# Tiles of 32 queries for the second pair of heads in block 1's attention, and w_a and w_b packed in place

## The chip, the cores and the metric
One core of a Trainium2 chip runs the kernel. Its engines take their instructions each from a list of its own: PE (TensorE: matrix products and transposes), DVE (VectorE), ACT (ScalarE) and POOL (GpSimd); SP and POOL also issue transfers. The lists are fixed when the program is built, and an instruction waits until what it needs is done, and with it all that stand behind it in its list. The metric is the time of one execution on the device, in microseconds. The granted clock of PE was 0.999 of full speed in the profiled execution, which is the level of 2.4 GHz.

## The reference
```python
def _attn_ref(q, k, v):                      # (4, 8, 576, 64) each
    scores = scale * np.matmul(q, k.transpose(0, 1, 3, 2))
    mask_local = (rel >= 0) & (rel < stride)               # stride = 32, heads 0 to 3
    mask_strided = (rel >= 0) & (pos[None, :] % stride == pos[:, None] % stride)   # heads 4 to 7
    ...                                      # softmax over the masked scores, sum + 1e-9
    return np.matmul(attn, v)
def _moe_ref(x, w_in, w_out, s, b):          # x (2304, 512), w_in (512, 2048), w_out (2048, 512)
    r = np.maximum(x @ w_in, 0.0)
    return (s * (r * r) + b) @ w_out
def _moe2_ref(x, w_a, w_b, w_out):           # w_a, w_b (512, 1536), w_out (1536, 512)
    return ((x @ w_a) * (x @ w_b)) @ w_out
```
The three run one after the other. The weights come as doubles (64 bits); the kernel converts them to 32-bit floats.

## The kernel before
Tokens are cut into blocks; the first network runs block by block over 16 steps f of its hidden units. One step ("call") of block n issues on PE twelve matmuls for h of step f (`h_mm`, into one PSUM bank of the pool ps_h), twelve matmuls acc of an earlier step (`o_mm`), and then `attend`, which runs what is due of the attention of block n+1. Each product is made of three passes: both operands are split into a high half `[:, 0]` (written by ACT) and a low half `[:, 1]` (DVE's subtraction), both by `split`, L121 to L124. So after h of a step ACT does relu (L802), the square (L806) and the high half "hi" of gt (L122), DVE then the low half "lo" (L124), and acc of that step stands two calls later.

In block 0 the weights w_in and w_out are converted in the same calls: `to_float32` (L140) takes two 32-bit words for each number, in a tile `raw`: ACT scales the high words (L142), DVE shifts the low ones (L145), joins them (L148) and packs the result (L158); `split` makes the halves w.

The attention of a block has four parts: two pairs of local heads (a band of 32 keys) and two pairs of strided heads. Each is a generator of six or seven steps: loads, transposes of queries and keys, scores, softmax, transposes of the probabilities (ppt), products with v (po). `plan` (L1059) gives each step its call by a table; the call's number in block 0 is first + t. `attend` puts a step's PE work behind that call's acc; DVE's and ACT's parts are put in place by the scheduler. There are two forms of each kind. `local` (L289) and `strided` (L371) work in tiles of 64 queries and transpose queries and keys on PE (pst); a `local` call covers four or three tiles, so each pair needs two. `local_pairs` (L453) and `strided_pairs` (L513) work in tiles of 32 queries over the whole block, transpose on DVE, and have half as many columns in the strided softmax (288 against 576). Before, block 1's attention, which runs beside block 0 of the network (44 to 137 us), is all in the first form; the blocks behind it use the second.

The softmax of `local` in block 1 puts the mask in by a PE matmul (mask times ident_b) and takes the sum with the exponential on ACT (accum_out); the other forms add the mask on DVE and sum on DVE.

In blocks 1 to 3 `convert_w2` (L851) converts the 36 words of the second network's w_a, w_b and w_out, i = 0 to 35, kind i % 3: `to_float32` packs word i into a tile w2s (one buffer), POOL stores it to w2d[i] (L865) and then loads word i+2 (L130 for w_a and w_b, L135 for w_out) into the pool raw, which has two buffers.

Of the kernel before, what the change touches and what calls it, by code (L numbers as in the profile page):

```python
# [10 lines left out]
F32 = mybir.dt.float32  # L11
F32R = mybir.dt.float32r
U32 = mybir.dt.uint32
BF16 = mybir.dt.bfloat16
AF = mybir.ActivationFunctionType
ALU = mybir.AluOpType
AX = mybir.AxisListType
# [3 lines left out]
P = 128  # L21
# [6 lines left out]
def sparse_attention_two_mlps(  # L28
# [14 lines left out]
    nc = tc.nc  # L43
    B, H, S, D = q.shape
    NT, DM = out.shape
# [7 lines left out]
    TF = P  # L53
# [9 lines left out]
    scale = 1.0 / float(D) ** 0.5  # L63
# [5 lines left out]
    hp = ctx.enter_context(tc.tile_pool(name="hp", bufs=1))  # L69
# [11 lines left out]
    lp = att.enter_context(tc.tile_pool(name="lp", bufs=1, side="right"))  # L81
# [11 lines left out]
    w2s = [dram.tile([P, 2, 2, DM], F32, name=f"w2s{i}") for i in range(NF2)]  # L93
# [4 lines left out]
    def mm(*args, **kwargs):  # L98
        last_pe[:] = [nc.tensor.matmul(*args, **kwargs).ins]  # L99
# [40 lines left out]
    def to_float32(r, out=None, quarters=False):  # L140
        low, high = r[:, :, 0], r[:, :, 1]
        nc.scalar.activation(  # L142
            out=high.bitcast(F32), in_=high.bitcast(F32), func=AF.Copy, scale=HIGH_SCALE
        )
        nc.vector.tensor_scalar(  # L145
            out=low, in0=low, scalar1=29, scalar2=None, op0=ALU.logical_shift_right
        )
        nc.vector.scalar_tensor_tensor(  # L148
            out=low, in0=high, scalar=3, in1=low, op0=ALU.logical_shift_left, op1=ALU.bitwise_or
        )  # L150
        out = high if out is None else out
        pieces_ = [(out, high, low)]
        if quarters:
            to = out.rearrange("p (r a i c) -> p a r i c", r=2, a=2, c=STR)
            low, high = (t.rearrange("p (r i a c) -> p a r i c", r=2, a=2, c=STR) for t in (low, high))
            pieces_ = [(to[:, a], high[:, a], low[:, a]) for a in range(2)]
        for to, high, low in pieces_:
            nc.vector.scalar_tensor_tensor(  # L158
                out=to, in0=high, scalar=0x80000000, in1=low, op0=ALU.bitwise_and, op1=ALU.bitwise_or
            )  # L160
        return out.bitcast(F32)
# [24 lines left out]
    QT = 64  # L186
# [246 lines left out]
    def softmax_pairs(pt, pss, msk, cols):  # L433
        na = pt.shape[1]
        wide = msk[:, None, None, :].to_broadcast([P, na, 2, cols])
        for h, of in enumerate((pt[:, :, 0:4:3, 0:cols], pt[:, :, 1:3, 0:cols])):
            nc.vector.tensor_tensor(
                out=of, in0=pss[h].rearrange("p (a b) c -> p a b c", b=2), in1=wide, op=ALU.add
            )
        pt = pt.rearrange("p a x c -> p (a x) c")[:, :, 0:cols]  # L440
        mx = lp.tile([P, 4 * na], F32, tag="mx", name="mx", bufs=2)
        sm = lp.tile([P, 4 * na], F32, tag="sm", name="sm", bufs=2)
        wide = lambda t: t[:, :, None].to_broadcast(list(pt.shape))
        nc.vector.tensor_reduce(out=mx, in_=pt, op=ALU.max, axis=AX.X)
        nc.vector.tensor_tensor(out=pt, in0=pt, in1=wide(mx), op=ALU.subtract)
        nc.scalar.activation(out=pt, in_=pt, func=AF.Exp, scale=scale)
        yield
        nc.vector.tensor_reduce(out=sm, in_=pt, op=ALU.add, axis=AX.X)
        nc.vector.tensor_scalar_add(out=sm, in0=sm, scalar1=1e-9)
        nc.vector.reciprocal(out=sm, in_=sm)  # L450
        nc.vector.tensor_tensor(out=pt, in0=pt, in1=wide(sm), op=ALU.mult)

    def local_pairs(bb, n, pair):  # L453

        nt = TR // QS
        nu = -(-nt // 4)
        nq, nk = TR, TR + STR
        room = lp.tile([P, nq + nk], F32, tag="qk", name="qk")
        qk = room.rearrange("p (j c) -> p j c", c=STR)
        pt = room[:, 0:nu * 2 * PITCH].rearrange("p (a x c) -> p a x c", x=4, c=PITCH)  # L460
        blocks_load(qk, 0, q, bb, 2 * pair, TF, S)
        blocks_load(qk, nt, k, bb, 2 * pair, TF - STR, S)
        yield
        qkT = lp.tile([P, nq + nk], F32, tag="lT", name="qkT")
        qT, kT = qkT[:, 0:nq], qkT[:, nq:]
        with after(list(behind)):
            nc.vector.transpose(out=qkT.rearrange("p (j c) -> p j c", c=STR), in_=qk)
        yield
        vn = [lp.tile([P, m, D], F32, tag=tag, name="vn") for m, tag in ((8, "vn"), (nt - 8, "lpt"))]
        for h in range(2):  # L470
            at = v[bb, 2 * pair + h, TF - STR:S, :]
            for u in range(nu):
                m = min(4, nt - 4 * u)
                p0 = (h ^ u % 2) * WS
                src = bass.AP(at.tensor, at.offset + 4 * u * QS * D, [[D, WS], [QS * D, m], [1, D]])
                nc.sync.dma_start(out=vn[u // 2][p0:p0 + WS, u % 2 * 4:u % 2 * 4 + m], in_=src)
        pss = [ps_a.tile([P, nu, WS], F32, tag="a", name="pss") for _ in range(2)]
        for j in range(4 * nu):
            i = min(j, nt - 1) * QS
            for h in range(2):  # L480
                hr = slice(h * D, (h + 1) * D)
                mm(
                    pss[h][j % 4 * QS:(j % 4 + 1) * QS, j // 4],
                    lhsT=qT[hr, i:i + QS], rhs=kT[hr, i:i + WS], start=True, stop=True,
                )
        yield from softmax_pairs(pt, pss, masks[QS][0], WS)
        yield
        ppt = ps_a.tile([P, nu, P], F32, tag="a", name="ppt")
        for u in range(nu):
            mm_t(ppt[:, u], pt[:, u // 2, u % 2 * 2:u % 2 * 2 + 2].rearrange("p x c -> p (x c)"), ident)  # L490
        pT = lp.tile([P, nu, P], F32, tag="lT", name="pT")
        nc.scalar.activation(out=pT, in_=ppt, func=AF.Copy)
        yield
        po = [ps_a.tile([P, nu // 2, P], F32, tag="a", name="po") for _ in range(2)]
        for a in range(nu // 2):
            for jj in range(4):
                for b in range(2):
                    u, c = 2 * a + b, slice(jj * QS, (jj + 1) * QS)
                    j = 4 * u + jj
                    for h in range(2 * (j < nt)):  # L500
                        rows = slice((h ^ b) * WS, (h ^ b) * WS + WS)
                        mm(
                            po[b][h * D:(h + 1) * D, a, c], lhsT=vn[a][rows, j - 8 * a], rhs=pT[rows, u, c],
                            start=True, stop=True,
                        )
        xt, c0 = x_tile(n), first_column(n)
        for u in range(nu):
            c1 = c0 + u * P
            m = min(P, c0 + nq - c1)
            split(xt[:, 0, pair, c1:c1 + m], xt[:, 1, pair, c1:c1 + m], po[u % 2][:, u // 2, 0:m])  # L510
        yield
# [339 lines left out]
    def convert_w2():  # L851
        words = {}

        def load(i):
            if i < 3 * NF2:
                f, kind = divmod(i, 3)
                words[i] = stage((w_a, w_b, w_o2)[kind], f, kind < 2, raw, nc.gpsimd)[0]

        load(0)
        load(1)  # L860
        yield
        for i in range(3 * NF2):
            with after(list(behind)):
                w = to_float32(words.pop(i), hp.tile([P, DM], U32, tag="w", name="w2s"), i % 3 == 2)
            nc.gpsimd.dma_start(out=w2d[i], in_=w)  # L865
            load(i + 2)
            yield
# [189 lines left out]
    steps = {}  # L1057

    def plan(n):  # L1059
        at_f = (-3, 0, 1, 2, 4, 5) if n == 1 else (-3, 0, 1, 2, 3, 5)  # L1060
        if n == 1:
            near = [
                (4 * i - 1, local(0, n, i % 2, TF + i // 2 * 4 * QT, 4 - i // 2), (-2, 0, 1, 1, 2, 3, 4))
                for i in range(4)
            ]
        else:
            near = [(8 * i, local_pairs(n - 1, n, i), (-5, -1, 0, 1, 2, 4)) for i in range(2)]
        far = [(8 * i + 1, (strided if n == 1 else strided_pairs)(n - 1, n, i), at_f) for i in range(2)]
        if n == 1:
            near[0] = (0, near[0][1], (-5, -3, 0, 1, 1, 2, 3))  # L1070
            far[0] = (1, far[0][1], (-5, 1, 2, 3, 5, 7))
        if n == 2:
            near[0] = (0, near[0][1], (-4, -1, 0, 1, 2, 4))
        for first_, gen, at in near + far:
            for t in at:
                steps.setdefault((n - 1) * NF1 + first_ + t, []).append(gen)
# [510 lines left out]
```

## Time and profile before
| | |
|---|---|
| median of 3 runs | 881.11 us (880.87 to 881.37) |
| the profiled execution | 882.01 us, span 880.2 us |
| PE busy | 870.9 us, 99% |
| DVE, ACT, POOL busy | 679.1, 406.4, 158.1 us |
| mean DMA rate over the span | 213 GB/s |
| chain that ended last | PE 96%, ACT 2%, DVE 1% |

The profiled execution is one of its own, 0.90 us above the median of the timed ones. Busy PE time is modelled at the ends of matmuls, so starts are the better mark. Engines other than PE are busy for part of the span, and their idle time costs nothing as long as PE doesn't wait for them.

### The profile page before, as it was taken

How to read it: one execution, taken by the hardware profiler on the slowest of the kernel's cores; microseconds unless marked ns; L12 is line 12 of the kernel's file. 1: busy time of each engine (PE TensorE's matmuls, PEld its weight loads, DVE VectorE, ACT ScalarE, POOL GpSimd, SP SyncE). 2: the span in 40 equal slices, each digit the busy share in tenths (PEclk: the TensorE clock that was granted, in tenths of full speed). 3: DMA queues.
4: the chain of work that ended last, by engine and by line, in shares of the span. 5: the costliest groups of instructions: out<-in, count | busy, mean ns of one | idle time of the engine just before them, and what ended most of it. 6: DMA issues, size and time to landing. Idle time of an engine off the chain costs nothing.

```text
span 880.2 us, 17207 instructions
## 1 busy us (share of the span) xinstructions
PE 870.9 (99%) x6296; PEld 805.4 (92%) x6296; DVE 679.1 (77%) x1363; ACT 406.4 (46%) x872; POOL 158.1 (18%) x308
## 2 busy tenths in 40 slices
PE   8999999999999999999999999999999999999998
PEld 6778888999888899998888999999999999999998
DVE  6898996686767676847876798798877797887794
ACT  6777774443433343337665333463223463222261
POOL 6000001111112211114544000005400005200020
PEclk9999999999999999999999999999999999999999
DMA  9975543866685758458999668688668788766487
GB/s 213 289 236 151 173 85 105 186 163 165 170 201 151 178 173 188 140 169 281 351 317 338 197 207 261 216 256 263 203 198 278 251 252 260 211 200 206 150 259 217
DMA packets 173156, 187.21 MB, mean 213 GB/s; under 512 B 108880, under 2 KB 125648, under 8 KB 173072
## 3 DMA queue, kind: packets, MB, share of 16 engines
q1 hardware_dynamic: 147776, 119.90, 47.7%
q0 software_dynamic: 20096, 64.90, 22.4%
q10 hardware_dynamic: 5200, 1.31, 0.8%
q8 instruction: 50, 0.82, 0.4%
q14 instruction: 34, 0.28, 0.1%
HBM read 143.59 MB, written 42.47 MB: 211 GB/s over the span
## 4 chain that ended last, share of the span: by engine, by line
PE 96%; ACT 2%; DVE 1%; issue 0%; POOL 0%; ACTq 0%; POOLq 0%
PE pp L99 30%; PE h L99 23%; PE acc L99 22%; PE o L99 15%; PE po L99 2%; PE pss L99 1%; PE ppt L102 1%; PE fpo L99 1%; ACT fpt L620 1%; PE lull L99 0%; ACT raw L142 0%; PE fps L102 0%; PE pst L102 0%; ACT fqkT L620 0%; PE fpp L102 0%; PE fss L99 0%
## 5 line engine op out<-in xcount | busy, mean ns | idle before, releaser
L99 PE MATMUL pp<-x2w,wf 128*128 128x384 f32 x1296 | 230.9, 334 | 0.0
L99 PEld LDWEIGHTS pp<-x2w,wf 128*128 128x128 f32 x1296 | 225.2, 188 | 0.1
L99 PE MATMUL h<-x,w 128*128 128x512 f32 (+1 forms) x960 | 215.8, 373 | 0.0
L99 PE MATMUL acc<-gt,w 128*128 128x512 f32 (+2 forms) x960 | 210.7, 368 | 1.0 <-ACT w L122 1.0
L99 PEld LDWEIGHTS acc<-gt,w 128*128 128x128 f32 x960 | 175.5, 188 | 24.0 <-ACT w L122 1.4
L99 PEld LDWEIGHTS h<-x,w 128*128 128x128 f32 x960 | 172.5, 188 | 24.5 <-DVE w L124 0.5
L99 PE MATMUL o<-gf,o2w 128*128 128x384 f32 (+1 forms) x756 | 130.3, 333 | 0.7 <-issue 0.7
L99 PEld LDWEIGHTS o<-gf,o2w 128*128 128x128 f32 x756 | 129.6, 188 | 1.1 <-ACT gf L620 1.0
L802 ACT ACTIVATE r<-h 128x512 f32<-128x512 f32 (+1 forms) x80 | 44.3, 554 | 134.3 <-PE h L99 121.3
L620 ACT ACTIVATE gf<-quad 128x384 fp32r<-128x384 f32 x126 | 63.6, 522 | 84.4 <-DVE quad L625 61.6
L1343 POOL DMA_DIRECT2D out_dram<-ot x80 | 44.7, 567 | 249.4 <-DVE ot L1329 242.0
L625 DVE TENSOR_TENSOR gf<-quad,gf 128x384 fp32r<-128x384 f32 x126 | 67.6, 551 | 7.1 <-ACT gf L620 5.2
L812 DVE TENSOR_TENSOR r<-r 128x384 f32<-128x384 f32 (+1 forms) x48 | 28.9, 602 | 56.0 <-ACT gt L809 56.0
L625 DVE TENSOR_TENSOR quad<-pp,quad 128x384 f32<-128x384 f32 x108 | 59.8, 554 | 10.1 <-PE pp L99 8.4
L865 POOL DMA_DIRECT2D w2d<-w2s x36 | 19.7, 548 | 182.3 <-DVE w2s L158 155.7
L142 ACT ACTIVATE raw<-raw 128x512 f32<-128x512 f32 x66 | 42.6, 669 | 7.2 <-DMA raw<-in_moe_w_a_dram 3.3
L148 DVE SCALAR_TENSOR_TENSOR raw<-raw 128x512 uint32<-128x512 uint32 x66 | 44.5, 690 | 1.1
L620 ACT ACTIVATE wf<-wsrc 128x512 fp32r<-128x512 f32 x30 | 18.9, 629 | 54.1 <-PE pp L99 38.1
L99 PE MATMUL pp<-x2w,wh 128*128 128x384 f32 x216 | 43.2, 334 | 0.0
L620 ACT ACTIVATE quad<-pp 128x384 f32<-128x384 f32 x36 | 17.6, 490 | 54.3 <-PE pp L99 54.3
L625 DVE TENSOR_TENSOR quad<-quad 128x384 f32<-128x384 f32 x72 | 39.9, 554 | 1.3
L99 PEld LDWEIGHTS pp<-x2w,wh 128*128 128x128 f32 x216 | 38.0, 188 | 0.0
(191 smaller groups left out, 1011.9 us busy)
## 6 DMA issues: line engine op xcount, KB each, us to landing
o2w<-w2o SPq DMA_DIRECT2D x126, 256.0 KB
wf<-w2s SPq DMA_DIRECT2D x60, 512.0 KB
w2d<-w2s POOLq DMA_DIRECT2D x36, 256.0 KB, 2.6
w2r<-w2d POOLq DMA_DIRECT2D x36, 256.0 KB, 5.0
raw<-in_moe_w_in_dram SPq DMA_DIRECT2D x16, 512.0 KB
raw<-in_moe_w_out_dram SPq DMA_DIRECT2D x16, 512.0 KB
wsrc<-w2d SPq DMA_DIRECT2D x30, 256.0 KB
raw<-in_moe_w_a_dram POOLq DMA_DIRECT2D x12, 512.0 KB, 5.1
```

Of the source, the lines that this page charges most:

```text
L99: last_pe[:] = [nc.tensor.matmul(*args, **kwargs).ins]
L102: last_pe[:] = [nc.tensor.transpose(*args).ins]
L142: nc.scalar.activation(out=high.bitcast(F32), in_=high.bitcast(F32), func=AF.Copy, scale=HIGH_SCALE)
L148: nc.vector.scalar_tensor_tensor(out=low, in0=high, scalar=3, in1=low, op0=ALU.logical_shift_left, op1=ALU.bitwise_or)
L620: i = nc.scalar.activation(**kwargs).ins
L625: i = getattr(nc.vector, method)(**kwargs).ins
L802: relu = nc.scalar.activation(out=r, in_=ph, func=AF.Relu)
L812: nc.vector.tensor_tensor(out=r, in0=r, in1=r, op=ALU.mult)
L865: nc.gpsimd.dma_start(out=w2d[i], in_=w)
L1343: engines[k % len(engines)].dma_start(out=at.rearrange("(j t) c -> t j c", t=STR), in_=st[i * STR:(i + 1) * STR, j:j + m].rearrange("t j a ...
```

## The change
Block 1's attention keeps the first form for pair 0 of the local and of the strided heads; pair 1 of both goes over to the second form. The calls are: the local pass of pair 0's last three tiles at 3 instead of 7; `local_pairs` of pair 1 with loads in call 4, DVE transposes in 8, scores in 9, the rest of the exponentials in 10, normalising in 11, ppt in 12, po in 13; `strided_pairs` of pair 1 with loads in 6, transposes in 9, scores in 11, normalising in 12, ppt in 13, po in 14. For this block `local_pairs` takes a new softmax, `sums_pairs`: mask by PE, maxima by DVE from PSUM, eight exponentials of 64 columns on ACT with the sum beside, four in one call and four in the next.

`convert_w2` now packs the words of w_a and w_b into the front of their own raw tile; only w_out's have the tile w2s.

```diff
+    def sums_pairs(pt, pss, _, cols):
...
+        for h in range(2):
+            nc.vector.tensor_reduce(out=mx[:, h], in_=pss[h], op=ALU.max, axis=AX.X)
+        nc.vector.tensor_scalar_mul(out=mx, in0=mx, scalar1=-scale)
+        for h in range(2):
+            if h:
+                yield
+            for u in range(2 * na):
+                a, x = u // 2, ((0, 3), (1, 2))[h][u % 2]
+                nc.scalar.activation(
+                    out=pt[:, a, x, 0:cols], in_=pss[h][:, u], func=AF.Exp, scale=scale,
+                    bias=mx[:, h, u:u + 1], accum_out=sm[:, a, x:x + 1],
+                )
+        yield
...
+        nc.vector.tensor_scalar_add(out=sm, in0=sm, scalar1=1e-9)
+        nc.vector.reciprocal(out=sm, in_=sm)
+        nc.vector.tensor_tensor(
+            out=pt, in0=pt, in1=sm[:, :, :, None].to_broadcast(list(pt.shape)), op=ALU.mult
+        )
...
     def local_pairs(bb, n, pair):
...
+        sums = n == 1
+        if sums:
+            wide = masks[QS][0][:, None, :].to_broadcast([P, nu, WS])
+            for h in range(2):
+                mm(pss[h], lhsT=ident_b, rhs=wide, start=True, stop=False)
...
-        yield from softmax_pairs(pt, pss, masks[QS][0], WS)
+        yield from (sums_pairs if sums else softmax_pairs)(pt, pss, masks[QS][0], WS)
...
-                w = to_float32(words.pop(i), hp.tile([P, DM], U32, tag="w", name="w2s"), i % 3 == 2)
+                r = words.pop(i)
+                if i % 3 == 2:
+                    w = to_float32(r, hp.tile([P, DM], U32, tag="w", name="w2s"), True)
+                else:
+                    w = to_float32(r, r.rearrange("p c t -> p (c t)")[:, 0:DM])
             nc.gpsimd.dma_start(out=w2d[i], in_=w)
             load(i + 2)
...
     def plan(n):
...
+                (8, local_pairs(0, n, 1), (-4, 0, 1, 2, 3, 4, 5)),
...
+                (9, strided_pairs(0, n, 1), (-3, 0, 2, 3, 4, 5)),
```

PE's list before, calls 12 to 15 of block 0 (h and acc are the network's products; ppt from spt and po from spT are strided pair 1's transposes and products, ppt from lpt and po from pT those of the local pass):

```order
L99 MATMUL h<-x,w 128x512 x12
L99 MATMUL acc<-gt,w 128x512 x12
L102 MATMUL ppt<-ident,spt 72x128 x8
L99 MATMUL h<-x,w 128x512 x12
L99 MATMUL acc<-gt,w 128x512 x12
L102 MATMUL ppt<-ident,lpt 96x128 x4
L99 MATMUL po<-spT,sv 64x14x4 x16
L99 MATMUL h<-x,w 128x512 x12
L99 MATMUL acc<-gt,w 128x512 x12
L99 MATMUL po<-pT,vn 64x64 x6
```

PE's list now, calls 11 to 14 (sqk holds the strided probabilities):

```order
L99 MATMUL h<-x,w 128x512 x12
L99 MATMUL acc<-gt,w 128x512 x12
L99 MATMUL pss<-sqkT 32x36 x32
L99 MATMUL h<-x,w 128x512 x12
L99 MATMUL acc<-gt,w 128x512 x12
L102 MATMUL ppt<-ident,qk 128x128 x4
L99 MATMUL h<-x,w 128x512 x12
L99 MATMUL acc<-gt,w 128x512 x12
L99 MATMUL po<-pT,vn 64x32 x28
L102 MATMUL ppt<-ident,sqk 128x128 x4
L99 MATMUL h<-x,w 128x512 x12
```

The strided scores of pair 1 stand in call 11 (in call 10 before), the transposes in call 13 (12 before), behind 28 products of the local pair. (The trace has two records for each matmul of scores and products: 28 here are 56 there.)

DVE's list before, around step 12's "lo" (gt from r, gt), with the normalising multiply of strided pair 1 (spt from spt, sm):

```order
L270 TENSOR_SCALAR sm<-sm 128x8
L158 SCALAR_TENSOR_TENSOR raw<-raw 128x512 x2
L271 RECIPROCAL sm<-sm 128x8
L124 TENSOR_TENSOR w<-raw,w 128x512
L272 TENSOR_TENSOR spt<-spt,sm 128x576
L124 TENSOR_TENSOR gt<-r,gt 128x512
L249 TENSOR_REDUCE mx<-pss 128x2
```

DVE's list now, around step 13's "lo", with the same pair's multiply (sqk from sqk, sm):

```order
L158 SCALAR_TENSOR_TENSOR raw<-raw 128x512
L450 RECIPROCAL sm<-sm 128x8
L124 TENSOR_TENSOR gt<-r,gt 128x512
L145 TENSOR_SCALAR raw<-raw 128x512 x2
L124 TENSOR_TENSOR w<-raw,w 128x512
L451 TENSOR_TENSOR sqk<-sqk,sm 128x8x36
L124 TENSOR_TENSOR w<-raw,w 128x512
```

The multiply that the transposes need has moved from ahead of a "lo" to behind one, and two shifts and a low half of a weight stand between.

POOL's list before, words 7 to 9 of the second network's weights, with the semaphores that each waits for:

```order
L865 DMA w2d_117<-w2s 128x512 [waits DMASW4_49,DVE_49]
L135 DMA raw<-in_moe_w_out_dram 128x1024 [waits DMASW1_49,Activation_49]
L865 DMA w2d_118<-w2s 128x512 [waits DMASW6_49,DVE_49]
L130 DMA raw<-in_moe_w_a_dram 128x4x256 [waits DMASW3_49,Activation_49]
L865 DMA w2d_119<-w2s 128x512 [waits DMASW0_49,DVE_49]
```

POOL's list now, words 9 to 11:

```order
L899 DMA w2d_117<-raw 128x512 [waits DMASW1_49,DMASW4_49,DVE_49,Activation_49]
L135 DMA raw<-in_moe_w_out_dram 128x1024 [waits DMASW4_49]
L899 DMA w2d_118<-raw 128x512 [waits DMASW3_49,DVE_49,Activation_49]
L130 DMA raw<-in_moe_w_a_dram 128x4x256 [waits DMASW6_49]
L899 DMA w2d_119<-w2s 128x512 [waits DVE_49]
```

Behind a store from raw (w2d_117, w2d_118) the next load waits for a transfer of POOL's own queue (DMASW4, DMASW6), which is that store; before, it waited for an earlier load and for ACT.

## Rows read from the trace of the kernel before
**Rows 1.** Page, part 1: busy time (share of the span) and instructions of each engine.
```profile
PE 870.9 (99%) x6296; PEld 805.4 (92%) x6296; DVE 679.1 (77%) x1363; ACT 406.4 (46%) x872; POOL 158.1 (18%) x308
```

**Rows 2.** Waits of PE, whole span: who waited for whom, total us, times, longest.
```profile
PE pss L99 <- ACT qkT L312: 0.7, 1, 0.7
```

**Rows 3.** Timeline of PE, block 0: start, duration, operation, count [idle before].
```profile
55.44 1.03 PE L99 MATMUL pss<-sqkT 64*64 64x72 f32 x32 [0.73 <-ACT qkT L312]
...
61.98 0.34 PE L99 MATMUL pss<-lmask,ident_b 128*128 128x192 bf16 x2
...
65.60 2.88 PE L99 MATMUL acc<-gt,w 128*128 128x512 f32 x12
...
71.04 2.89 PE L99 MATMUL acc<-gt,w 128*128 128x512 f32 x12
...
77.85 2.88 PE L99 MATMUL acc<-gt,w 128*128 128x512 f32 x12
...
111.58 2.88 PE L99 MATMUL acc<-gt,w 128*128 128x512 f32 x12
...
120.63 1.05 PE L102 MATMUL ppt<-ident,spt 128*72 128x128 f32 x8
...
127.55 1.15 PE L99 MATMUL po<-spT,sv 72*64 72x56 f32 x32
...
131.48 2.88 PE L99 MATMUL acc<-gt,w 128*128 128x512 f32 x12
```

**Rows 4.** Windows of 22 us: busy us (instructions) of each engine, clock, DMA share, GB/s.
```profile
110.00:132.00 22.00, 22.00 (x141) 17.79 (x140) 20.94 (x46) 15.42 (x35) 0.92 (x1) 1.00 0.44 85
```

**Rows 5.** Timeline of PE, block 3, the same columns.
```profile
264.62 2.88 PE L99 MATMUL acc<-gt,w 128*128 128x512 f32 x12
...
291.64 1.12 PE L99 MATMUL po<-pT,vn 64*64 64x32 f32 x56
...
308.24 2.88 PE L99 MATMUL acc<-gt,w 128*128 128x512 f32 x12
```

**Rows 6.** Timeline of ACT around step 11 of block 0.
```profile
111.78 0.60 ACT L802 ACTIVATE r<-h 128x512 f32<-128x512 f32 x1 [1.35 <-DVE x L124]
...
114.47 0.64 ACT L122 ACTIVATE gt<-r 128x512 fp32r<-128x512 f32 x1
```

**Rows 7.** Timeline of DVE, block 0 and (last row) block 3.
```profile
115.23 0.75 DVE L272 TENSOR_TENSOR spt<-spt,sm 128x576 f32<-128x576 f32 x1
...
123.16 0.68 DVE L124 TENSOR_TENSOR gt<-r,gt 128x512 fp32r<-128x512 f32 x1
123.77 0.76 DVE L145 TENSOR_SCALAR raw<-raw 128x512 uint32<-128x512 uint32 x2
...
284.39 0.46 DVE L451 TENSOR_TENSOR sqk<-sqk,sm 128x288 f32<-128x288 f32 x1
```

**Rows 8.** Landing times of the stores L865, then of the loads L135 on POOL.
```profile
DMA to landing us min/median/max: 2.3/2.6/6.5
...
DMA to landing us min/median/max: 4.1/4.9/6.2
```

**Rows 9.** Timeline of all engines, block 3, around one word.
```profile
329.48 0.55 POOL L865 DMA_DIRECT2D w2d<-w2s  x1 [2.34 <-DVE w2s L158]
...
330.02 0.54 POOL L135 DMA_DIRECT2D raw<-in_moe_w_out_dram  x1
...
335.72 0.70 ACT L142 ACTIVATE raw<-raw 128x512 f32<-128x512 f32 x1 [0.99 <-DMA raw<-in_moe_w_out_dram]
...
338.45 0.69 DVE L148 SCALAR_TENSOR_TENSOR raw<-raw 128x512 uint32<-128x512 uint32 x1
...
339.57 0.76 DVE L158 SCALAR_TENSOR_TENSOR w2s<-raw 128x256 uint32<-128x256 uint32 x2 [0.42 <-DMA w2d<-w2s]
...
340.94 0.49 ACT L802 ACTIVATE r<-h 128x384 f32<-128x384 f32 x1
...
341.48 0.80 PE L99 MATMUL h<-x,w 128*128 128x384 f32 x3
```

More of the change, by code (lines that the diff above doesn't have):

```diff
@@ L451, in softmax_pairs @@
         nc.vector.tensor_tensor(out=pt, in0=pt, in1=wide(sm), op=ALU.mult)
+    def sums_pairs(pt, pss, _, cols):
+        na = pt.shape[1]
+        mx = lp.tile([P, 2, 2 * na], F32, tag="mx", name="mx", bufs=2)
+        sm = lp.tile([P, na, 4], F32, tag="sm", name="sm", bufs=2)
+        for h in range(2):
[11 more added lines that the diff above has]
+        yield
+        pt = pt[:, :, :, 0:cols]
+        nc.vector.tensor_scalar_add(out=sm, in0=sm, scalar1=1e-9)
[3 more added lines that the diff above has]
+        )
     def local_pairs(bb, n, pair):
@@ L483, in local_pairs @@
                     pss[h][j % 4 * QS:(j % 4 + 1) * QS, j // 4],
-                    lhsT=qT[hr, i:i + QS], rhs=kT[hr, i:i + WS], start=True, stop=True,
+                    lhsT=qT[hr, i:i + QS], rhs=kT[hr, i:i + WS], start=not sums,
+                    stop=(not sums or j >= 4 * nu - 4),
                 )
-        yield from softmax_pairs(pt, pss, masks[QS][0], WS)
+        yield from (sums_pairs if sums else softmax_pairs)(pt, pss, masks[QS][0], WS)
         yield
@@ L1059, in plan @@
     def plan(n):
-        at_f = (-3, 0, 1, 2, 4, 5) if n == 1 else (-3, 0, 1, 2, 3, 5)
         if n == 1:
             near = [
-                (4 * i - 1, local(0, n, i % 2, TF + i // 2 * 4 * QT, 4 - i // 2), (-2, 0, 1, 1, 2, 3, 4))
-                for i in range(4)
+                (0, local(0, n, 0, TF, 4), (-5, -3, 0, 1, 1, 2, 3)),
+                (3, local(0, n, 0, TF + 4 * QT, 3), (-2, 0, 1, 1, 2, 3, 4)),
+                (8, local_pairs(0, n, 1), (-4, 0, 1, 2, 3, 4, 5)),
+            ]
+            far = [
+                (1, strided(0, n, 0), (-5, 1, 2, 3, 5, 7)),
+                (9, strided_pairs(0, n, 1), (-3, 0, 2, 3, 4, 5)),
             ]
@@ L1067, in plan @@
             near = [(8 * i, local_pairs(n - 1, n, i), (-5, -1, 0, 1, 2, 4)) for i in range(2)]
[L1068 to L1071, printed above, removed]
+            far = [(8 * i + 1, strided_pairs(n - 1, n, i), (-3, 0, 1, 2, 3, 5)) for i in range(2)]
         if n == 2:
```

## The prediction
> **What bounds the kernel now.** Four views, in this order. The page's first part gives each engine's share: PE is busy nearly the whole span, the others are not [rows 1]. The last wait of PE for another engine is that for pss, 0.7 us, at 55.44 [rows 2, 3], so in the stretch behind it that the change touches the end is set by the sum of PE's work: work taken from PE there comes off the time, and work moved to DVE or ACT costs nothing until PE waits for it. The timeline of PE is read from the start of one group to the start of the next, since ends of matmuls are modelled. Block 0 repeats "12 matmuls acc, 12 matmuls h"; where nothing lies between, acc to acc is 71.04 − 65.60 = 5.44 us [rows 3]. What a call has over 5.44 us is its price of attention. Last come the windows, ACT and DVE: DVE is busy 20.94 of 22 us there [rows 4], so an operation that PE needs can come late although DVE is "only" 77% busy over the span.
>
> **Part one, PE's work in block 0 (block 1's attention).** Calls 0 to 2 keep their instructions. In calls 3 to 6 one of the transposes of a key or query block drops out (−0.1 us). The local pass of pair 0 in call 7 keeps the product that stood in call 15 before; these cancel. Calls 7 to 14 of before run from acc at 77.85 to acc at 131.48 [rows 3]: 53.63 us, of which eight plain calls are 8 × 5.44 = 43.52, so attention costs 10.11 us. What takes its place in calls 8 to 14:
> - one local_pairs and one strided_pairs as they stand in block 3, also with 512 columns: acc 264.62 to acc 308.24 is 43.62 us, less seven plain calls (38.08) is 5.54 us [rows 5]. That holds scores, transposes and products of both;
> - two mask matmuls over 256 columns before the scores; two over 192 take 0.34 us together [rows 3], so 0.3 to 0.45; I take 0.3, since the next group begins before the modelled end;
> - scores of the strided pair and transposes of the local pair now stand in two calls and not in one, so h and acc are interrupted once more: 0.1 us;
> - the product of strided pair 0, which keeps its place in call 8: 1.15 busy, 1.1 to the next group [rows 3].
> Sum 7.04. PE's work falls by 10.11 − 7.04 + 0.1 = 3.2 us. Bounds: 2.4 to 4.0 us, an error of 0.1 us at each of the eight places where attention and h or acc meet in calls 7 to 14, in one direction.
>
> **The wait that it adds.** In the new order the strided pair's scores stand in call 11 and its transposes in call 13, behind acc of step 11 and 28 products of the local pair. The transposes need the normalising multiply on DVE. That one stood ahead of "lo", the low half of gt, in the list before, and now stands behind the "lo" of step 13, two shifts of raw and one low half of a weight. DVE and ACT take their lists in order, so from the end of h of step 13:
> - ACT: relu, two conversions of raw, one w, square, "hi". For step 11 the same six stand between relu at 111.78 and "hi" at 114.47, which lasts 0.64; h ends about when acc starts, at 111.58 [rows 3, 6]: 3.53 us to the end of "hi";
> - DVE: "lo" 123.16 to 123.77 = 0.61, two shifts 0.76 busy, 0.67 without the 0.08 by which a row of this kind runs on into the next, w 0.61 as "lo", which has its shape, the multiply over 288 columns 0.46 [rows 7]: 2.35 us. The chain is 5.88 us.
> - PE meanwhile has acc, half of a plain call = 2.72 us, and 28 products, 1.12 busy, 1.1 [rows 5]: 3.8 us.
> PE so waits 5.88 − 3.8 = 2.1 us ahead of the transposes. What is queued behind them on PE is h of step 14 and so every later call; nothing catches up, since PE is the bound. Before, the multiply started at 115.23 and its transposes at 120.63 [rows 3, 7], 4.6 us after its end; with half the columns the multiply is shorter by 0.3 us (0.75 to 0.46), but the call that gave the 4.6 us is gone. Bounds: 1.6 us, if products and acc run 0.2 us longer each; 2.7 us, since DVE has 1.06 us free in 22 [rows 4] and may come to "lo" some tenths late. I take 2.2.
>
> **Other changes of the attention, at nothing.** The bank that exponentials leave (call 9 to 10, eight of 64 columns in two calls) is not asked for before call 11, more than 5 us later, and ACT has work taken away. The transposes on DVE stand a call or more ahead of the scores, and DVE loses about as much in adds, maxima and multiplies over twice the columns as it gets in transposes. SP issues more loads of short rows in front of the weights. No wait of PE, ACT or DVE for w_in or w_out is in the trace behind 56 us, so a delay of a few us there is covered; if it weren't, PE would lose what the load is late.
>
> **Part two, words packed in place.** The words of w_a and w_b stay in their raw tile, so POOL may only load word i+2 over word i when the store of w2d[i] has landed. A store lands after 2.6 us in the median, 6.5 at most [rows 8]; before, the load went out 0.54 us behind it (329.48, 330.02) [rows 9]. Two loads of three go out about 2.1 us later. DVE's wait of 0.42 us for w2d at 339.57 goes. The place with the least room is that one: ACT waited 0.99 us for this word at 335.72, DVE packed at 339.57, then come ACT's halves of x, relu at 340.94, and h of PE at 341.48, which takes the one bank that relu frees. From the store at 329.48 the word now needs 2.6 + 5.7 (the load of then, 330.02 to 335.72) = 8.3 us, so ACT starts at 337.8, 2.1 later. In the new list "hi" stands ahead of this conversion on ACT, so DVE's squares don't wait for it. DVE's second step on the word, at about 338.45, needs ACT's result at 338.4: it comes out just in time, and the 0.42 us saved are the whole margin [rows 9]. So 0 to 1 us; I take 0.3.
> The Trainium skill, page "DMA: Bandwidth & Descriptors", section "Anatomy of one DMA — SWDGE (gpsimd) path", puts such a transfer at about 2.0 us plus its bytes at 436 GB/s. For the store of 256 KB that makes 2.6 us, which the trace has; for the load of 512 KB 3.2 us, where the trace has 4.9 in the median [rows 8]. By the page store and load would take 5.8 us of the 8.3, and this term would be 0.
>
> **Sum.** −3.2 + 2.2 + 0.3 = −0.7 us. Against the profiled execution's 882.01 us (span 880.2) that is 881.3; the median of the runs shown, 881.11, lies 0.90 lower, so 880.4 us. The range of this case: −4.0 + 1.6 = −2.4 to −2.4 + 2.7 + 1 = +1.3, that is 878.7 to 882.4.
>
> **Rivals.**
> - *The multiply is in time.* Then PE keeps all: −3.2 + 0.3 = −2.9, 878.2 us. For it: PE had no wait in this stretch before, and block 3 runs the same routine without one. Against it: there the multiply starts at 284.39, and the transposes stand behind products that start at 291.64 [rows 5, 7], since DVE converts no weights of the first network in block 3. Each term of the chain has a row, and 2 us would have to be wrong.
> - *Late words hold PE (slower).* A store and its load may together take longer than 8.3 + 0.4 = 8.7 us at the place above; from there each us passes through ACT, DVE and relu to h. With the longest landings seen, 6.5 + 6.2 = 12.7 [rows 8], it costs 4.0 us: 880.4 + 4.0 = 884.4. For it: ACT waits for these words already. Against it: 2.6 + 4.9 = 7.5 in the median, and in most places the words lie longer.
> - *The change doesn't shorten PE's work*, since the small tiles of block 0 cost as much as those that they replace: −3.2 falls to 0, the wait stays: +2.5, 883.6. Against it: the 5.54 us of block 3 are the same instructions.
>
> **Chances.** Forecast 0.62; multiply in time 0.22; late words 0.11; no shorter work 0.05. This measurement can tell 0.2%, 1.76 us, from no change: faster is under 879.35, slower over 882.87. Faster: 0.21 of the first rival and 0.06 of the forecast, whose low end lies under that bound, 0.27. Slower: 0.10 + 0.04 + 0.01, 0.15. The rest, 0.58, is the same. The range for 8 in 10 goes down to 877.7, the first rival's middle with a little more work saved, and up to 883.4, part of the way to late words.
>
> **What would show it.** In PE's waits of after, one new line: transposes (L102) waiting for the multiply (sqk) by 1.6 to 2.7 us, once, near 120 us. Acc of call 7 to acc of call 14 should take 53.6 − 3.1 + 2.2 = 52.7 us. In blocks 1 to 3 ACT's waits for raw grow, and PE has no wait, or one for relu under 1 us. Wrong would be: no line for sqk; a PE wait at the scores of local_pairs or for w; or a gap of PE for relu or h in blocks 1 to 3 of several us.

## The result and the profile after
| | before | after |
|---|---|---|
| median | 881.11 us (880.75 to 881.37, 5 runs) | 888.65 us (886.45 to 891.46, 5 runs) |
| profiled execution, span | 882.01, 880.2 us | 891.46, 889.7 us |

The ratio is 1.0087 (95% interval 1.0068 to 1.0105): slower by 7.5 us where 0.7 us less was forecast, and the runs now lie 5 us apart; the one profiled is the slowest of the five. The busy times hardly moved (after, page, part 1; [rows 1] for before):

```profile
PE 872.2 (98%) x6395; PEld 804.5 (90%) x6395; DVE 678.1 (76%) x1361; ACT 404.2 (45%) x866; POOL 158.4 (18%) x308
```

PE's waits of after, three of its lines (total, times, longest); before had none of them, the last wait there for another engine was that for pss [rows 2]:

```profile
PE ppt L102 <- issue: 4.1, 2, 2.6
...
PE pss L99 <- DVE qkT L491: 2.6, 2, 2.0
PE h L99 <- ACT r L832: 1.5, 4, 0.5
```

The first is the forecast wait at the strided transposes, and a second one like it; the other two are new kinds, and a wait at the scores of `local_pairs` (pss from qkT) is one of the signs by which the prediction said that it would be wrong. In block 0 the timeline of PE shows the forecast stall, and one row that nobody had counted (after, PE):

```profile
42.64 3.02 PE L99 MATMUL acc<-gt,w 128*128 128x512 f32 x12 [1.01 <-ACT w L122]
...
114.57 2.88 PE L99 MATMUL acc<-gt,w 128*128 128x512 f32 x12
117.38 1.12 PE L99 MATMUL po<-pT,vn 64*64 64x32 f32 x56
121.06 0.63 PE L102 MATMUL ppt<-ident,sqk 128*128 128x128 f32 x4 [2.56 <-issue]
121.45 4.59 PE L99 MATMUL h<-x,w 128*128 128x512 f32 x12
125.87 2.91 PE L99 MATMUL acc<-gt,w 128*128 128x512 f32 x12
...
137.60 2.92 PE L99 MATMUL acc<-gt,w 128*128 128x512 f32 x12
```

PE waits 2.56 us ahead of the transposes at 121.06, where 2.2 were forecast. But the twelve matmuls of h behind them take 4.59 us where their like takes 3.02. The windows of that place (PE's busy time first, PEclk third from the right) show the clock with it:

```profile
114.57:121.06 6.49, 3.93 (x69) 3.10 (x68) 6.49 (x16) 4.89 (x10) 0.00 (x0) 1.00 0.42 75
121.06:125.87 4.81, 4.80 (x16) 3.87 (x17) 4.33 (x10) 1.95 (x5) 0.91 (x1) 0.65 0.64 169
```

The granted clock is 1.00 up to the end of the stall and 0.65 in the 4.8 us behind it: for a part of these PE is at the lower of its two levels, 1.2 GHz, after it stood idle. ACT's "hi" and DVE's rows are those of the forecast, in its order (after; "hi", "lo", and behind two shifts and a w the multiply):

```profile
117.61 0.63 ACT L122 ACTIVATE gt<-r 128x512 fp32r<-128x512 f32 x1
...
118.68 0.65 DVE L124 TENSOR_TENSOR gt<-r,gt 128x512 fp32r<-128x512 f32 x1
...
120.51 0.46 DVE L451 TENSOR_TENSOR sqk<-sqk,sm 128x288 f32<-128x288 f32 x1
```

From the first acc of block 0 to the first acc with the narrower h behind it, before took 137.00 − 43.23 = 93.77 us (kernel before, PE):

```profile
43.23 3.02 PE L99 MATMUL acc<-gt,w 128*128 128x512 f32 x12 [1.01 <-ACT w L122]
...
137.00 2.92 PE L99 MATMUL acc<-gt,w 128*128 128x512 f32 x12
```

After takes 137.60 − 42.64 = 94.96. So block 0 is 1.2 us longer: the stall 2.56, the slow h 1.57, and PE's work 2.9 less.

The larger part is lost in blocks 1 to 3. PE's waits there add up to 5.7 us, where before has none. ACT's waits for raw words, before and then after (total, times, longest):

```profile
ACT raw L142 <- DMA raw<-in_moe_w_a_dram: 3.3, 4, 1.7
...
ACT raw L142 <- DMA raw<-in_moe_w_b_dram: 2.9, 2, 1.6
...
ACT raw L142 <- DMA raw<-in_moe_w_out_dram: 1.0, 1, 1.0
```

```profile
ACT raw L142 <- DMA raw<-in_moe_w_a_dram: 22.0, 10, 3.3
ACT raw L142 <- DMA raw<-in_moe_w_out_dram: 20.2, 7, 5.8
...
ACT raw L142 <- DMA raw<-in_moe_w_b_dram: 5.9, 5, 1.9
```

From 7 us to 48. One such place of after, in order of time, all engines:

```profile
262.49 0.54 POOL L135 DMA_DIRECT2D raw<-in_moe_w_out_dram  x1 [3.32 <-DMA w2d<-raw]
...
263.02 0.55 POOL L899 DMA_DIRECT2D w2d<-raw  x1
...
266.08 2.88 PE L99 MATMUL acc<-gt,w 128*128 128x512 f32 x12
...
267.25 0.66 ACT L142 ACTIVATE raw<-raw 128x512 f32<-128x512 f32 x1 [5.81 <-DMA raw<-in_moe_w_out_dram]
267.81 0.61 ACT L839 ACTIVATE gt<-r 128x512 fp32r<-128x512 f32 x1
...
268.46 0.69 DVE L842 TENSOR_TENSOR r<-r 128x512 f32<-128x512 f32 x1 [4.05 <-ACT gt L839]
...
269.79 1.14 DVE L491 STREAM_TRANSPOSE qkT<-qk 128x928 f32<-128x928 f32 x1
...
270.98 0.86 PE L99 MATMUL pss<-qkT 64*32 64x64 f32 x64 [2.02 <-DVE qkT L491]
...
271.77 4.60 PE L99 MATMUL h<-x,w 128*128 128x512 f32 x12
...
276.21 2.90 PE L99 MATMUL acc<-gt,w 128*128 128x512 f32 x12
```

POOL may issue the load of a w_out word only at 262.49, having waited 3.32 us for a store to land. ACT waits 5.81 us for the word, and "hi" (267.81) stands behind it in ACT's list. DVE waits 4.05 us for "hi" at 268.46, and the transposes of queries and keys (L491) stand behind DVE's squares: the scores wait 2.02 us, and the clock falls again, so that h takes 4.60 us. From acc to acc this call takes 276.21 − 266.08 = 10.13 us, in before 271.11 − 264.62 = 6.49, 3.6 us less. The store at 263.02 itself held the next load until 268.19. The window of that h, in the columns of the two above:

```profile
271.77:276.21 4.44, 4.44 (x19) 3.50 (x13) 3.61 (x8) 1.20 (x2) 1.29 (x2) 0.62 0.35 101
```

### The profile page after: what moved, and what is told of

It is laid out like the page before. It is cut to its first block, busy times and chain, and to the rows that moved or that the text cites. A ratio compares the mean times of both kernels' runs of the same rounds, so it can differ in the third digit from the quotient of the medians.

```text
span 889.7 us, 17433 instructions
## 1 busy us (share of the span) xinstructions
PE 872.2 (98%) x6395; PEld 804.5 (90%) x6395; DVE 678.1 (76%) x1361; ACT 404.2 (45%) x866; POOL 158.4 (18%) x308
## 4 chain that ended last, share of the span: by engine, by line
PE 87%; DMA 5%; ACT 3%; DVE 2%; issue 2%; SPq 1%; POOL 0%; ACTq 0%; POOLq 0%; DVEq 0%
PE pp L99 29%; PE h L99 20%; PE acc L99 18%; PE o L99 15%; DMA raw<-in_moe_w_b_dram 2%; PE po L99 2%; PE pss L99 1%; DMA raw<-in_moe_w_out_dram 1%; PE ppt L102 1%; DMA fqk<-in_k_dram 1%; PE fpo L99 1%; ACT raw L142 1%; DMA w2d<-raw 1%; DMA vn<-in_v_dram 1%; ACT r L832 0%
## 5 line engine op out<-in xcount | busy, mean ns | idle before, releaser
L99 PE MATMUL h<-x,w 128*128 128x512 f32 (+1 forms) x960 | 219.4, 378 | 1.5 <-ACT r L832 1.5
L99 PEld LDWEIGHTS h<-x,w 128*128 128x128 f32 x960 | 174.9, 190 | 28.0 <-ACT r L832 3.0
L148 DVE SCALAR_TENSOR_TENSOR raw<-raw 128x512 uint32<-128x512 uint32 x66 | 44.6, 692 | 2.5 <-ACT raw L142 1.4
L158 DVE SCALAR_TENSOR_TENSOR raw<-raw 128x512 uint32<-128x512 uint32 x54 | 36.2, 688 | 0.5
```

Source lines behind the costliest of these rows:

```text
L148: nc.vector.scalar_tensor_tensor(out=low, in0=high, scalar=3, in1=low, op0=ALU.logical_shift_left, op1=ALU.bitwise_or)
L158: nc.vector.scalar_tensor_tensor(out=to, in0=high, scalar=0x80000000, in1=low, op0=ALU.bitwise_and, op1=ALU.bitwise_or)
```

## The experiments
All were timed beside the kernel before, whose medians on those chips were 880.45 to 881.05 us.

**The attention part alone.** Packing as before, all else as changed:
```diff
-                else:
-                    w = to_float32(r, r.rearrange("p c t -> p (c t)")[:, 0:DM])
+                w = to_float32(words.pop(i), hp.tile([P, DM], U32, tag="w", name="w2s"), i % 3 == 2)
```


> Only the attention part; the words go through w2s as before. Theory A (two losses that add up: the stall ahead of the strided transposes with the slow clock behind it in block 0, and late words in blocks 1 to 3): the stall of about 2.5 us and one h group at the low clock (4.6 instead of 3.0 us) stay, PE has no wait in blocks 1 to 3, and the time is 881.1 + 1.2 = 882.3 us (881.8 to 882.9). Rival B (the words are slow only because block 0 ends later): the waits of blocks 1 to 3 stay in part, 884 to 886 us. Rival C (the slow clock comes from elsewhere): no slow group, 880.5 us.

882.35 us (880.92 to 883.96, 7 runs), 1.0025 [1.0013, 1.0036]: in A's range. The execution profiled was the fastest of the seven; in it the stall is there, the slow group isn't, and PE has one wait in blocks 1 to 3, 0.64 us for relu at 341.43, where A had none (PE):

```profile
121.15 0.63 PE L102 MATMUL ppt<-ident,sqk 128*128 128x128 f32 x4 [2.61 <-issue]
121.53 3.00 PE L99 MATMUL h<-x,w 128*128 128x512 f32 x12
```

So the stall is in both profiles, and the clock fell behind it in after's and not in this one. The mean granted clock of the seven executions says the same of the others: four have 0.996 to 0.998 and took 882.25 to 883.96 us, three have 0.999 or 1.000 and took 880.92, 882.06 and 882.35. The median is one of these three, so that it falls on A's 882.3, which has a slow group in it, is in part luck.

**The words alone.** The kernel before with the packing of after.

> Only the words in place; block 1's attention as before. Theory A: the larger loss, 886 to 888 us, with PE waits behind DVE's transposes, relu and a normalising multiply in blocks 2 and 3, and ACT waiting 30 us or more for raw words. Rival B (no loss without the change in block 0): 881 to 882 us. By the forecast on record (0 to 1 us) 881.1 to 882.1.

886.84 us (885.85 to 888.30), 1.0070 [1.0057, 1.0083]. The words cost 5.8 us without any change in block 0; B and the forecast on record are out. The execution profiled (885.85) has four waits of PE in blocks 1 to 3, where before has none, and a slow h behind the last:

```profile
341.60 2.36 PE L99 MATMUL h<-x,w 128*128 128x384 f32 x12 [0.55 <-ACT r L802]
...
356.54 0.86 PE L99 MATMUL pss<-qkT 64*32 64x64 f32 x64 [0.77 <-DVE qkT L467]
...
362.14 2.37 PE L99 MATMUL h<-x,w 128*128 128x384 f32 x12 [0.35 <-ACT r L802]
...
368.15 0.63 PE L102 MATMUL ppt<-ident,qk 128*128 128x128 f32 x4 [1.56 <-issue]
...
369.40 3.91 PE L99 MATMUL h<-x,w 128*128 128x384 f32 x12
```

The waits add up to 3.2 us, and h at 369.40 takes 3.91 us where its like takes 2.33, at a granted clock of 0.65 from 368.15 to 373.00. Together these are 4.8 us, which is what this execution has over the median of before (881.05).

**The transposes a call later.** The attention part alone, with
```diff
-                (9, strided_pairs(0, n, 1), (-3, 0, 2, 3, 4, 5)),
+                (9, strided_pairs(0, n, 1), (-3, 0, 2, 3, 5, 6)),
-        for kk in (0, 2, 3, 1) if n and f == 0 else range(KD):
+        for kk in ((0, 2, 1, 3) if n == 1 else (0, 2, 3, 1)) if n and f == 0 else range(KD):
```


> The attention part alone, with the strided pair's transposes in call 14 and products in call 15, and block 1's first h taking that quarter of x last. Theory A: the multiply is done a call before its transposes; stall and slow group both go, PE's saved work is left: 881.1 - 3.1 = 878.0 us (877.6 to 878.8). If the saved work had been put too high, 879 to 881; if the wait only moves to block 1's first h, a PE wait of 1 us or more there and 879 us or more.

879.42 us (877.11 to 879.97, 11 runs), 0.9981 [0.9972, 0.9989]: faster than before, but by 1.6 us and not 3.1. The stall and the slow group are gone. Of the 1.5 us that are missing 0.8 stand in one line of PE's waits and in three rows of DVE and ACT at the place that the prediction had named as the tightest [rows 9]:

```profile
PE h L99 <- ACT r L832: 0.8, 1, 0.8
```

```profile
337.67 0.76 DVE L158 SCALAR_TENSOR_TENSOR w2s<-raw 128x256 uint32<-128x256 uint32 x2 [1.94 <-DMA w2d<-w2s]
...
338.67 0.48 ACT L122 ACTIVATE x<-po 128x64 fp32r<-128x64 f32 x2 [3.51 <-DVE x L124]
...
339.04 0.48 ACT L832 ACTIVATE r<-h 128x384 f32<-128x384 f32 x1
```

DVE waits 1.94 us for the single w2s tile (0.42 before), ACT's third piece of x waits for DVE, relu stands behind it, and PE's h waits for relu.

**The stall filled.** The attention part alone, with matmuls ahead of the transposes whose sums these overwrite:
```diff
+        for _ in range(9 if n == 1 else 0):
+            mm(ppt.rearrange("p g t -> p (g t)"), lhsT=ident_b, rhs=..., start=True, stop=True)
```


> The attention part alone, with nine bf16 matmuls of 512 columns (about 1.9 us) put ahead of the strided transposes of call 13, where PE stands idle; their sums are overwritten by the transposes. Theory A (the idle PE lowers the clock): the wait is filled, h of step 14 keeps 3.0 us, the time is 1.6 us under that of the attention part alone, 880.7 us. Rival D (the slow group has another cause): h of step 14 still 4.6 us, 882.3 us or more.

880.80 us (879.76 to 881.32, 11 runs), 1.55 us under the attention part alone. The granted clock is 0.999 or 1.000 in each of the eleven executions, where four of seven were lower without the filling; D is out. PE's rows:

```profile
118.55 2.12 PE L99 MATMUL ppt<-lmask,ident_b 128*128 128x512 bf16 x9
121.16 0.66 PE L102 MATMUL ppt<-ident,sqk 128*128 128x128 f32 x4 [0.49 <-DVE sqk L451]
121.57 3.00 PE L99 MATMUL h<-x,w 128*128 128x512 f32 x12
```

The transposes start no earlier than without the filling (121.16 against 121.15), so the stall is as long; in this profile only its clock can be saved. The clock isn't all of the 1.55 us, since two executions of the attention part alone took 882.06 and 882.35 at a clock of 1.000; what the rest comes from isn't shown.

**Which words.** The kernel before with only w_a's words in place, and then with only w_b's:
```diff
+                if i % 3 == 0:    # the other run: == 1
+                    w = to_float32(r, r.rearrange("p c t -> p (c t)")[:, 0:DM])
```


> Before, with only w_a's 12 words in place: each load of a w_out word then waits for a store. Theory A1 (a raw tile's round of load, turn on ACT and DVE, and store no longer fits two words' pace when two words of three are held longer; with one of three the next tile comes early enough to make it up): a loss clearly under half of the 5.8 us measured for both, 881.1 to 883. Rival (each delayed load costs by itself, wherever the word is needed at once): about half or more, 884 to 886, since w_out's words are those with the longest ACT waits.

> Before, with only w_b's 12 words in place: each load of a w_a word waits for a store, and the w_out word behind no longer waits for the w2s tile (0.42 us of DVE in the trace of before, near 339 us). Theory A1: little, 880.5 to 882.5, the wait for w2s gone and no PE wait over 0.5 us. Rival (each delayed load costs by itself): 883 to 885.

w_a alone 881.00 us, 1.0003 [0.9994, 1.0012]; w_b alone 882.29 (880.30 to 885.61), 1.0018 [1.0008, 1.0028]. Together they cost 5.8, so the costs don't add: nearer to A1 than to the rival, and the wait for w2s near 339 us is gone as A1 had it; but w_b's cost is at the upper end of A1's range, and PE waits twice for 1.2 us where A1 had none over 0.5. ACT's waits for the words whose load was held, of the one and of the other:

```profile
ACT raw L142 <- DMA raw<-in_moe_w_out_dram: 7.2, 6, 2.1
```

```profile
ACT raw L142 <- DMA raw<-in_moe_w_a_dram: 23.8, 10, 3.9
```

**Stores on another queue.** Both kinds in place, with `nc.sync.dma_start(out=w2d[i], in_=w)` for POOL's.

> Both kinds in place, as in the run with the words alone (886.84), but the stores go out on SP's queue and not on POOL's. If much of the loss is the store of word i+1 standing behind a load that waits for store i on POOL, the loss halves: 883 to 884.5 us. If it is the round of the raw tile alone, 886 to 888; SP's own loads may be held by a store that waits, which adds to either.

890.87 us (889.31 to 893.89), 1.0117: worse by 4 us, more than either branch gave, so this told nothing of POOL's queue by itself. Two of ACT's waits for raw words (4.8 and 3.7 us) end in its trace with attention loads of SP; whether the 4 us come from these isn't shown.

**One or some words in place beside the later transposes.** First w_b's, then word 28 alone (`if i == 28:`).

> The attention part with its transposes a call later (879.42 measured), and w_b's words in place. The profile of that kernel lost 0.8 us of PE near 338 us, where DVE waits 1.94 us for the w2s tile's store. If that wait is the cause, it goes: 878.0 to 878.8 us. If the delayed loads of w_a cost as much or more: 879.4 to 882.

> The attention part with its transposes a call later (879.42 measured), and word 28 alone packed in place, so that word 29 doesn't wait for the w2s tile. If that wait (1.94 us of DVE in that kernel's profile, 0.8 us of PE) costs what it shows, 878.3 to 878.8 us. If the load of word 30, which now waits for a store, gives it back further on: 879.4 or more.

880.36 us (878.55 to 886.93) and 879.72 (878.56 to 881.07): no gain on 879.42. With word 28 alone PE no longer waits near 338 us, but loses 0.8 us at a normalising multiply and 0.6 behind DVE's transposes further on, as the second branch of its expectation had it.

**The whole change with the transposes a call later.**

> The whole change, with only the strided transposes a call later as in the run at 879.42. Theory A (the two losses add): the words' 5.8 us stay, the stall and the slow group of block 0 go: 879.4 + 5.8 = 885.2 us (884.5 to 886.2). Rival (the words are late because block 0 stalls): under 882 us.

883.51 us (881.74 to 890.24, 9 runs). Not 885.2: most of the loss stays, so the rival is out, but the two losses are not a plain sum, and the runs lie 8.5 us apart. The words cost 4.1 us here (883.51 − 879.42).

**x's high halves first.** The later transposes, packing as before, and in `local_pairs`
```diff
-            split(xt[:, 0, pair, c1:c1 + m], xt[:, 1, pair, c1:c1 + m], po[u % 2][:, u // 2, 0:m])
+        for u, c1, m in cuts:
+            nc.scalar.activation(out=xt[:, 0, pair, c1:c1 + m], in_=po[u % 2][:, u // 2, 0:m], func=AF.Copy)
+        for u, c1, m in cuts:
+            nc.vector.tensor_tensor(out=xt[:, 1, pair, c1:c1 + m], ..., op=ALU.subtract)
```


> The attention part with its transposes a call later (879.42 measured), and in local_pairs all four high halves of x on ACT ahead of the four low halves on DVE, so that ACT's third piece no longer waits for DVE, and relu not behind it. If PE's 0.8 us near 338 us come through that wait, PE's wait for relu there goes and the time is 878.2 to 878.8 us. If PE waits there for something else, 879.2 to 879.7.

877.93 us (877.25 to 878.43, 5 runs), 0.9966 [0.9953, 0.9979]: 2.5 us faster than before and the best of all. On the run without the new order it gains 1.5 us from median to median, and 0.9 when each is compared with the kernel before on its own chip (880.45 here, 881.05 there). The rows of the same place:

```profile
333.30 0.73 ACT L539 ACTIVATE x<-po 128x128 fp32r<-128x128 f32 x4
...
336.16 0.49 ACT L836 ACTIVATE r<-h 128x384 f32<-128x384 f32 x1 [1.54 <-PE h L99]
...
336.88 0.76 DVE L158 SCALAR_TENSOR_TENSOR w2s<-raw 128x256 uint32<-128x256 uint32 x2 [1.16 <-DMA w2d<-w2s]
...
338.04 2.24 PE L99 MATMUL h<-x,w 128*128 128x384 f32 x12
```

DVE still waits, 1.16 us for the tile, but ACT has its four pieces done at 334.0, relu waits only for PE's own h, and PE's waits have no line for relu left.

**The same with both kinds in place.**

> The same with both kinds of words in place (883.51 without the new order of x). Late words reach PE by several ways: relu behind x on ACT, DVE's transposes and the normalising multiply behind a late word. If they all count, only the first goes, and 881.5 to 883.0 us are left; if relu behind x was the only one, 878.5 to 879.5.

884.00 us (880.71 to 886.21, 11 runs), over the range of either branch, and 6.1 us over the same without the words. The new order of x gains nothing beside late words (883.51 without it), so relu behind x wasn't the main way by which they cost. In PE's waits of the execution profiled, the fastest of the eleven, 0.4 us are left for relu, and the multiply and the transposes:

```profile
PE ppt L102 <- issue: 1.7, 1, 1.7
...
PE pss L99 <- DVE qkT L491: 0.6, 1, 0.6
```

## Why the prediction was wrong
**The term that failed is "Part two, words packed in place", 0 to 1 us, taken as 0.3: it is 5.8 us** by the run with the words alone. The step in it that failed is "The place with the least room is that one". The price was worked out at one place, by what one late word does to relu there, and the others were taken to have room. That place came out as priced: with the words alone PE waits 0.55 us for relu at 341.60. What the runs show in place of the step is three more places, 0.77 us at the scores, 0.35 at relu and 1.56 at the transposes, and the clock that falls behind the last, 1.6 us.

A late word reaches these by more ways than relu. The prediction had "hi" ahead of the word's conversion on ACT; at 267.25 in after it stands behind it, squares on DVE behind "hi", and behind these DVE's transposes. With the words alone ACT waits 3.16 us for a w_out word at 359.17, whose load had waited 2.16 us for a store; DVE waits 2.01 us for "hi" at 360.28, and the normalising multiply, further down DVE's list at 367.36, is late for the transposes at 368.15. The rival "Late words hold PE" had this mechanism with a chance of 0.11 and a price of 4.0 at one place; each run of after lies above the range.

Why the words come late so often is argued from rows and not shown. One account is the rate: a word in place lengthens the round of a raw tile, and there are two tiles. From before (stores of all words, first and last start; and the store of word 29, whose load went out at 330.02 [rows 9]):

```profile
L865 POOL DMA_DIRECT2D w2d<-w2s x36: 547/547/560, 153.2 to 377.5; - x36
...
340.64 0.55 POOL L865 DMA_DIRECT2D w2d<-w2s  x1 [1.55 <-DVE x L124]
```

A word comes every (377.5 − 153.2) / 35 = 6.4 us, so a tile has 12.8 us for its round. The round of word 29 took 340.64 − 330.02 = 10.6 us from load to store. A word in place adds the landing of its store, in the median of after

```profile
DMA to landing us min/median/max: 2.3/3.2/5.8
```

so 3.2 us, more than before's 2.6. That makes 13.8 us for two words of three and 12.7 in the mean of the three, where there are 12.8: no room is left, so a word that is late stays late. With one kind in place two rounds of three stay as they were, which fits a cost of 0.3 or 1.5 us. No run changed the pace or the number of tiles. Rate alone doesn't cover all: word 28 alone, one held word of 36, is enough for PE waits of 0.6 us at the scores and 0.8 at the transposes behind them. And POOL takes its list in order, so the store of a w_b word stands behind a load that waits for w_a's store, as at 262.49 and 263.02 in after; no run tells what this adds.

By an estimate from the figures of the Trainium skill, page "DMA: Bandwidth & Descriptors", section "Anatomy of one DMA — SWDGE (gpsimd) path", this term would have been 0. After doesn't agree with them: 3.2 us in the median for a store where they make 2.6, 4.0 to 5.8 by kind of word for a load where they make 3.2.

**PE's saved work, forecast 3.2 us**, came out at 2.9. **The wait, forecast 2.2**, came out at 2.56, by the forecast chain; DVE came to "lo" at 118.68, 0.44 us after "hi" had ended, which was the reason given for the upper bound. **What no step held** is the clock behind the stall: 1.57 us in after's block 0 (h 4.59 for 3.02), and 1.55 from median to median between the attention part and the same with the stall filled, of which the clock is only a part. So "−3.2 + 2.2" is +1.3 in the median. In the execution profiled, in which the clock held, it is −0.1, and 0.64 us of what is missing there went at relu behind the w2s tile.

**"Other changes of the attention, at nothing" held** for the loads on SP, DVE's transposes of block 1 and the split exponentials: no PE wait in block 0 but the ones told. One cover was thinner than the text had it: DVE's wait for w2s, which took 0.42 us in before, takes 1.2 to 1.9 in the runs with the attention part and packing as before, and cost PE 0.3 to 0.8 us of the saved work until x was reordered.

**What stays open**: why the words cost 5.8 us in the kernel before, 6.3 beside the stall (888.65 − 882.35), 4.1 beside the later transposes and 6.1 there with x reordered; what part the pace of the tiles and the order of POOL's list each have in it; and why the clock falls in some executions with the same stall and not in others.

## What to carry to other kernels
A buffer that is held longer is priced at every place where its users wait, not only at the one with the least room, and its round is compared with the pace at which the buffers are asked for: here two holds that cost 0.3 and 1.5 us apart cost 5.8 together. Where PE is the bound, a stall of a few us is priced with the clock behind it. Before a wait is filled or moved, look at what only stands in the queue behind a waiting instruction: here the order of eight copies was worth 0.9 to 1.5 us.

## What the runs showed of the hardware
After a stall of 2.0 to 2.6 us PE ran the next twelve matmuls of 512 columns in 4.6 us and not 3.0, at a granted clock of 0.65 over 4.8 us (0.62 over 4.4 at the second place), with acc behind them at 2.9 again; with the words alone a stall of 1.56 us was enough (twelve of 384 columns in 3.91 us and not 2.33), and in after a like stall of 1.56 us at 374.15 left the clock at 1.00. With 2.1 us of other matmuls in the stall of block 0 no execution of eleven had a mean granted clock under 0.999, without them four of seven had. Stores of 256 KB took 2.3 to 6.5 us to land in one execution, and their median was 2.6 us in before and 3.2 in after, with the same bytes to move.
